# A decode kernel without its closing barrier, with its first transfers ahead of the entry barrier and w2 read in other pieces

## The chip, the core and the metric

The kernel runs on one core of one Trainium2 chip. The metric is the device time of one execution in microseconds (us). Beside it stands the *span* of a trace: the time from the first to the last instruction that the profile records. The time is a little longer than the span.

## The reference, cut to what matters

```python
x = A_x                                        # (8, 1, 576), bf16
g = sigmoid((x * gate_w).sum(-1))
# A: attention of one token over the last 2048 positions of a cache, 32 heads over 16 kv heads
q = x @ wq;  p = softmax(q @ k_cache[:, :, -2048:].T * 128**-0.5);  a = (p @ v_cache[:, :, -2048:]) @ wo
# B: an MLP
b = gelu(layernorm(x) @ w1 + b1) @ w2 + b2     # w1: (576, 4608), w2: (4608, 576)
out = g * a + (1 - g) * b                      # (8, 1, 576)
```

With 8 rows of activations there is little arithmetic. The two caches (8 x 16 x 2048 x 128 values each) and the weights have to come from HBM once: 154 MB.

## The kernel before

The kernel is a list of operations with dependencies, which a small planner puts in order for each engine and gives semaphores. SP issues nearly all transfers. They go into nine buffers of 16 KB in each partition, and one is issued as soon as the buffer that it needs is free.

```python
with ExitStack() as es:
    block = es.enter_context(nc.Block())         # closes with a barrier of all engines
    ...
    d_x   = dma("act", lambda e: e.dma_start(x_sb, x2), "x", ...)            # first transfer of ACT
    d_wqr = dma("sp", lambda e: e.dma_start(wq_r, A_wq[512:576, :]...), "wq", ...)  # first of SP
    d_wqm = dma("sp", lambda e: e.dma_start(wq_m..., A_wq[0:512, :]...), ...)       # second of SP
    ...
    # the last reads of the stream: w2, four blocks of 1152 rows, 9 rows to a partition
    src = B_w2[FCW * ci:FCW * ci + FCW, :].rearrange("(p j) n -> p (j n)", j=FJ)
    cuts = [0, 4, 7, 9] if ci == FC - 1 else [0, FJ]
    for n, (j0, j1) in enumerate(zip(cuts, cuts[1:])):
        d = dma("sp", lambda e: e.dma_start(dst[:, j0 * D:j1 * D], src[:, j0 * D:j1 * D]), ...)
        mms = [(hT[:, FJ * ci + j, :], dst[:, j * D:(j + 1) * D]) for j in range(j0, j1)]
        ...                                      # two matmuls of 288 columns for each row
    # then: two copies out of PSUM (DVE, ACT), two output transfers (SP, ACT), and
    add("sp", lambda e: None, deps=fin, name="final_wait", cost=0.05)

    P.schedule()
    @block.sync
    def _(e):
        P.emit("sp", e, eng_sems, dma_sems)
    ...                                          # the same for the other four engines
```

A program also begins with an entry barrier that is not in this text: each engine drains, GpSimd (POOL) sets four constants, and a semaphore releases all of them.

Of the kernel before, what the change touches and what calls it, by code (L numbers as in the profile page):

```python
# [12 lines left out]
ENGS = ("sp", "act", "pool", "dve", "pe")  # L13
# [25 lines left out]
class _Plan:  # L39
# [16 lines left out]
    def dma(self, eng, fn, semkey, nbytes, deps=(), name=None, after=(), prio=0):  # L56
        op = _Op(eng, fn, deps, name, self.DMA_ISSUE, after=after, is_dma=True, dma_sem=semkey, nbytes=nbytes, prio=prio)
        op.idx = len(self.all)
        self.all.append(op)
        return op  # L60
# [104 lines left out]
def _pst(t):  # L165
    return t.ap().ap[0][0]
# [13 lines left out]
def run_dma(nc, e, out, in_, shape=None):  # L180
    item = 2
    kw = {}
    if shape is not None:
        pst = shape[0]
        walk = shape[1]
        enc = []
        for step, num in reversed(walk[:-1]):
            parts, rest = divmod(step, pst)
            assert parts == 0 or rest == 0
            enc += [parts * 262144 + rest * item, num]  # L190
        enc += [0, 1] * (4 - len(enc) // 2)
        kw = dict(dst_dge_shape=enc, bass_dst_dge_shape=tuple(walk))
    return e.add_instruction(mybir.InstDMACopy(
        name=nc.get_next_instruction_name(), engine=e.engine, queue="qSPDynamicHW", mode="Copy",
        ins=e.lower_ap_dma(in_), outs=e.lower_ap_dma(out), **kw))


def build_kernel(nc, A_x, A_k_cache, A_v_cache, A_wq, A_wo, B_x, B_w1, B_b1, B_w2, B_b2, gate_w, out):
    B, Sq, D = A_x.shape
    _, Hkv, Sk, Dh = A_k_cache.shape  # L200
    Hq = A_wq.shape[1] // Dh
    F = B_w1.shape[1]
# [9 lines left out]
    FC, FJ = 4, 9  # L212
    FT = FC * FJ
    FCW = 128 * FJ
# [6 lines left out]
    out2 = out.rearrange("b s d -> (b s) d")  # L221

    with ExitStack() as es:
        block = es.enter_context(nc.Block())

        R = {}
        aoff = [0]

# [59 lines left out]
        AST = _pst(arena)  # L288
# [54 lines left out]
        def slot(s):  # L343
            return RAW[:, s * SE:(s + 1) * SE]
# [20 lines left out]
        eng_sems = {e: es.enter_context(nc.semaphore("sem_" + e)) for e in ENGS}  # L365
        dma_keys = ["x", "b", "b2", "wq", "w1", "out", "outb"] + ["s%d" % i for i in range(NSLOT)] + ["t%d" % i for i in range(4)]
        dma_sems = {k: es.enter_context(nc.semaphore("dma_" + k)) for k in dma_keys}

        P = _Plan()
        add, dma = P.add, P.dma  # L370
# [226 lines left out]
        def take_slot():  # L597
            n = n_slot[0]
            n_slot[0] += 1
            return (n + 6) % NSLOT  # L600
# [157 lines left out]
        def m2_chunk(ci):  # L758
            s = take_slot()
            dst = slot(s)[:, 0:FJ * D]  # L760
            src = B_w2[FCW * ci:FCW * ci + FCW, :].rearrange("(p j) n -> p (j n)", j=FJ)
            cuts = [0, 4, 7, 9] if ci == FC - 1 else [0, FJ]
            ops = []
            for n, (j0, j1) in enumerate(zip(cuts, cuts[1:])):
                d = dma("sp", (lambda j0=j0, j1=j1: lambda e: e.dma_start(dst[:, j0 * D:j1 * D], src[:, j0 * D:j1 * D]))(),  # L765
                        ("t%d" % n) if ci == FC - 1 else ("s%d" % s), 128 * (j1 - j0) * D * 2, deps=slot_free[s] if n == 0 else [], name="d_w2_%d_%d" % (ci, n), after=last_dma[-1:])
                last_dma.append(d)
                mms = [(hT[:, FJ * ci + j, :], dst[:, j * D:(j + 1) * D]) for j in range(j0, j1)]
                ops.append(AccGroup("m2_%d_%d" % (ci, n), mms, [o_hT, d], cost=0.25 * (j1 - j0), after=o_m2[-1:]).op)
                o_m2.append(ops[-1])  # L770
            slot_free[s] = ops

        pv_hist = []
        for kind, i in stream:
            {"K": k_unit, "V": v_unit, "W": wo_chunk, "M": m2_chunk, "B": bias}[kind](i)
# [11 lines left out]
        add("sp", lambda e: None, deps=fin, name="final_wait", cost=0.05)  # L787

        P.schedule()
        @block.sync  # L790
        def _(e):
            P.emit("sp", e, eng_sems, dma_sems)

        @block.gpsimd
        def _(e):
            P.emit("pool", e, eng_sems, dma_sems)

        @block.vector
        def _(e):
            P.emit("dve", e, eng_sems, dma_sems)  # L800

        @block.tensor
        def _(e):
            P.emit("pe", e, eng_sems, dma_sems)

        @block.scalar
        def _(e):
            P.emit("act", e, eng_sems, dma_sems)

    return P  # L810

# [1 line left out]
def bass_gated_mix__sliding_block_cached__mixer_channel_mlp__decode_kernel(  # L813
    nc: bass.Bass,
    A_x: bass.AP,
    A_k_cache: bass.AP,
    A_v_cache: bass.AP,
    A_wq: bass.AP,
    A_wo: bass.AP,
    B_x: bass.AP,  # L820
    B_w1: bass.AP,
    B_b1: bass.AP,
    B_w2: bass.AP,
    B_b2: bass.AP,
    gate_w: bass.AP,
    out: bass.AP,
):
    build_kernel(nc, A_x, A_k_cache, A_v_cache, A_wq, A_wo, B_x, B_w1, B_b1, B_w2, B_b2, gate_w, out)
# [28 lines left out]
```

## Time and profile before

| | before |
|---|---|
| time, median of the first 3 runs | 369.21 us |
| span of the profiled run, and its time | 367.5 us, 369.27 us |
| bytes read, mean rate over the span | 154 MB, 421 GB/s |
| busy: PE, DVE | 69%, 57% |

The first view is the DMA part of the profile. The digits are the busy share of the 16 DMA engines in 40 equal slices of the span, in tenths (9 is 90% or more); below them stands what they moved.

```profile
DMA  8999999999999999999999999999999999999994
GB/s 345 428 408 428 428 427 433 432 426 432 435 430 432 422 427 430 432 439 431 426 430 428 422 438 427 430 426 428 433 430 430 428 431 426 433 428 432 418 424 191
DMA packets 11851, 154.59 MB, mean 421 GB/s; under 512 B 1292, under 2 KB 1332, under 8 KB 3000
```

Between the ends the stream runs at about 430 GB/s without a hole. So the time is: when the stream starts, plus bytes over rate, plus what follows the last byte. Only the first slice (345) and the last (191) leave something to gain.

The start, from the timeline of SP's queue (start and duration in us, engine, line, what) and from the windows view (a stretch in us, its length, busy time of PE, PE's weight loads, DVE, ACT, POOL, then PE's clock, DMA share and GB/s):

```profile
0.79 0.39 SPq L401 DMA_DIRECT2D arena<-in_A_wq_dram  x1
1.24 0.42 SPq L402 DMA_DIRECT2D arena<-in_A_wq_dram  x1
1.70 0.42 SPq L404 DMA_DIRECT2D arena<-in_B_w_dram  x1
...
1.10:1.70 0.60, 0.00 (x0) 0.00 (x0) 0.00 (x0) 0.00 (x0) 0.56 (x3) 1.00 0.00 0
1.70:2.30 0.60, 0.00 (x0) 0.00 (x0) 0.00 (x0) 0.00 (x0) 0.59 (x5) 1.00 0.82 150
```

Nothing is issued for 0.79 us, and nothing moves until about 1.7 us.

The tail, from the chain of waits that ended last (start, duration, what):

```profile
297.09 32.53 DMA arena<-in_A_v_cache_dram
329.62 0.04 issue
329.66 1.08 PE ps L700 x16
...
333.71 30.42 DMA arena<-in_B_w_dram
364.13 0.04 issue
364.18 0.53 PE ps L559 x6
364.71 0.02 issue
364.73 0.43 PE ps L559 x4
...
365.28 0.45 DVE arena L783
```

The second piece of w2's last block (three rows, six matmuls) releases PE at 364.13; the last piece (two rows, four matmuls) follows. The same moments on PE's weight loads, whose bracket gives the idle time before them and what ended it:

```profile
364.17 0.22 PEld L559 LDWEIGHTS ps<-arena 128*8 128x8 bf16 x6 [0.97 <-DMA arena<-in_B_w_dram]
364.73 0.09 PEld L559 LDWEIGHTS ps<-arena 128*8 128x8 bf16 x4 [0.34 <-DMA arena<-in_B_w_dram]
```

And the end, from the records of the line that opened the closing block (first and last start in us); the output transfer of SP is issued at 365.75:

```profile
L223 SPq COMPARE_BRANCH  x1: 42/42/42, 367.1 to 367.1; - x1
L223 SPq DRAIN  x1: 13/13/13, 367.3 to 367.3; - x1
L223 SPq EVENT_SEMAPHORE  x1: 17/17/17, 367.5 to 367.5; - x1
L223 ACTq EVENT_SEMAPHORE  x1: 17/17/17, 367.5 to 367.5; - x1
```

The view of SP's waits shows (us in total, times, longest):

```profile
SPq L223 <- DMA out_dram<-arena: 0.2, 1, 0.2
```

The packed trace holds the times of *landing signals*: 16 for a large transfer, as many as there are DMA engines. That each signal is that of one engine is inferred from this number. In this trace the waits end with the last of them (the chain's 329.62 and 364.13 are such last signals). The views print no single signals, so they were read from the file. ACT's half of the output landed at 366.92, SP's half at 367.12.

### The profile page before, as it was taken

Reading aid. Unit: us, or ns where it says so; the run is one execution under the profiler, and the core shown is the slowest. Engines: PE = TensorE matmul, PEld = TensorE weight load, DVE = VectorE, ACT = ScalarE, POOL = GpSimd, SP = SyncE. Lnnn points to the kernel's source line nnn. Section 1 sums busy time; section 2 is a strip of 40 time slices with the busy share of each in tenths; the row PEclk is TensorE's granted clock in tenths of the full one; section 3 lists DMA queues with packets and bytes.
Section 4 is the critical chain, followed back from the end, with each engine's and each line's share of the span. In section 5 each row is a group of like instructions: output and inputs, shape, how many; then the busy total and the mean of one; then the engine's idle time right before and its main releaser. Section 6 shows DMA issues by size and latency. Waiting matters only on the chain.

```text
span 367.5 us, 4111 instructions
## 1 busy us (share of the span) xinstructions
PE 254.8 (69%) x1815; PEld 87.3 (24%) x1429; DVE 210.1 (57%) x253; ACT 47.8 (13%) x117; POOL 37.6 (10%) x163
## 2 busy tenths in 40 slices
PE   0349982895598398673986397765966396865995
PEld 0339200131123032010321032111311031214552
DVE  0704699797667754459654764478544864473000
ACT  1010002100300310003000300003100300003200
POOL 7020010011012001000101001010101000000000
PEclk9999998799689879887898879696988789795559
DMA  8999999999999999999999999999999999999994
GB/s 345 428 408 428 428 427 433 432 426 432 435 430 432 422 427 430 432 439 431 426 430 428 422 438 427 430 426 428 433 430 430 428 431 426 433 428 432 418 424 191
DMA packets 11851, 154.59 MB, mean 421 GB/s; under 512 B 1292, under 2 KB 1332, under 8 KB 3000
## 3 DMA queue, kind: packets, MB, share of 16 engines
q1 hardware_dynamic: 11776, 154.29, 98.6%
q8 instruction: 13, 0.21, 0.2%
q10 hardware_dynamic: 56, 0.03, 0.1%
q14 instruction: 6, 0.05, 0.0%
HBM read 154.31 MB, written 0.01 MB: 420 GB/s over the span
## 4 chain that ended last, share of the span: by engine, by line
DMA 74%; DVE 12%; PE 11%; SPq 1%; ACT 1%; issue 1%; DVEq 0%; ACTq 0%
DMA arena<-in_A_k_cache_dram 50%; DMA arena<-in_B_w_dram 15%; DMA arena<-in_A_v_cache_dram 9%; DVE arena L660 9%; PE ps L173 5%; PE ps L516 2%; PE ps L677 1%; DVE arena L605 1%; PE ps L700 1%; SPq L765 1%; ACT arena L619 1%; DVE arena L624 1%; PE ps L518 1%; PE ps L715 1%; DVE arena L614 0%
## 5 line engine op out<-in xcount | busy, mean ns | idle before, releaser
L660 DVE STREAM_TRANSPOSE arena<-arena 128x2048 f32<-128x2048 f32 x64 | 145.2, 2297 | 78.9 <-DMA arena<-in_A_k_cache_dram 71.5
L173 PE MATMUL ps<-arena 128*128 128x512 bf16 x401 | 134.4, 445 | 15.3 <-DVE arena L660 9.8
L677 PE MATMUL ps<-arena 128*128 128x512 bf16 x115 | 51.8, 450 | 16.7 <-DVE arena L660 16.6
L709 ACT ACTIVATE arena<-ps 128x512 f32<-128x512 f32 x32 | 19.1, 598 | 196.7 <-PE ps L700 196.7
L677 PEld LDWEIGHTS ps<-arena 128*128 128x128 bf16 x128 | 14.6, 114 | 125.8 <-issue 66.8
L715 PE MATMUL ps<-arena 128*128 128x8 f32 x256 | 36.9, 275 | 8.7 <-ACT arena L709 7.7
L653 POOL COPY arena<-arena 32x32 bf16<-32x32 bf16 x128 | 26.0, 203 | 159.2 <-PE ps L173 144.6
L715 PEld LDWEIGHTS ps<-arena 128*128 128x128 f32 x256 | 35.6, 217 | 22.4 <-ACT arena L709 16.4
L700 PE MATMUL ps<-arena 128*32 128x512 bf16 x512 | 36.7, 413 | 6.0 <-DMA arena<-in_A_v_cache_dram 6.0
L669 PE MATMUL ps<-arena 128*128 128x512 bf16 x6 | 3.5, 585 | 37.8 <-DVE arena L624 37.8
L605 DVE TENSOR_REDUCE arena<-ps 128x1 f32<-128x2048 f32 x8 | 18.3, 2282 | 15.5 <-PE ps L173 15.5
L619 ACT ACTIVATE arena<-ps,arena 128x512 bf16<-128x512 f32 x32 | 21.6, 686 | 41.4 <-DVE arena L614 41.4
L700 PEld LDWEIGHTS ps<-arena 128*32 128x32 bf16 x512 | 11.3, 100 | 39.8 <-issue 24.1
L624 DVE STREAM_TRANSPOSE arena<-arena 128x512 bf16<-128x512 bf16 x32 | 19.8, 674 | 0.9 <-ACT arena L619 0.9
L733 POOL TENSOR_TENSOR arena<-arena 128x16 bf16<-128x16 f32 x15 | 4.0, 267 | 142.3 <-ACT arena L725 142.3
L516 PE MATMUL ps<-arena 128*128 128x8 bf16 x144 | 10.9, 201 | 4.5 <-DMA arena<-in_B_w_dram 4.5
L559 PE MATMUL ps<-arena 128*8 128x288 bf16 (+1 forms) x140 | 11.6, 315 | 1.9 <-DMA arena<-in_B_w_dram 1.7
L516 PEld LDWEIGHTS ps<-arena 128*128 128x128 bf16 x144 | 10.8, 159 | 5.0 <-DMA arena<-in_B_w_dram 5.0
L669 PEld LDWEIGHTS ps<-arena 128*128 128x128 bf16 x8 | 0.9, 107 | 45.1 <-DVE arena L624 45.1
L733 DVE TENSOR_TENSOR arena<-ps,arena 128x16 bf16<-128x16 f32 x1 | 0.2, 229 | 19.4 <-PE ps L715 19.4
L438 PE MATMUL ps<-arena 8*128 8x8 bf16 x8 | 0.5, 168 | 13.5 <-DVE arena L411 9.8
L631 DVE RECIPROCAL arena<-ps 128x32 f32<-128x32 f32 x8 | 2.9, 358 | 10.5 <-PE ps L629 10.5
(83 smaller groups left out, 95.6 us busy)
## 6 DMA issues: line engine op xcount, KB each, us to landing
arena<-in_A_k_cache_dram SPq DMA_DIRECT2D x32, 2048.0 KB, 35.8
arena<-in_A_v_cache_dram SPq DMA_DIRECT2D x32, 2048.0 KB, 36.7
arena<-in_B_w_dram SPq DMA_DIRECT2D x1, 4608.0 KB, 24.3
arena<-in_A_wq_dram SPq DMA_DIRECT2D x1, 4096.0 KB, 13.1
arena<-in_B_w_dram SPq DMA_DIRECT2D x3, 1296.0 KB, 33.9
arena<-in_B_w_dram SPq DMA_DIRECT2D x2, 576.0 KB, 28.7
arena<-in_A_wq_dram SPq DMA_DIRECT2D x1, 512.0 KB, 3.7
arena<-in_B_w_dram SPq DMA_DIRECT2D x1, 432.0 KB, 30.4
```

The lines of the kernel that those rows point to most:

```text
L173: return e.add_instruction(mybir.InstMatmult(name=nc.get_next_instruction_name(), engine=mybir.EngineType.PE, ins=[e.lower_ap(rhs), e.lowe ...
L516: ins = e.matmul(out_, lhsT, yT[:, kt, :], start=(kt == 0), stop=False)
L559: ins = e.matmul(ps[32 * j:32 * j + 8, BK_ACC, 0:JN], lhsT, rhs[:, JN * j:JN * j + JN], start=False, stop=True, skip_group_check=True, til ...
L605: mx = add("dve", lambda e: e.tensor_reduce(out=k(MX), in_=ps[:, 0:4, :].rearrange("p a n -> p (a n)"), axis=AXL.X, op=ALU.max), deps=[qk_ ...
L619: return e.activation(out=Pm[:, 512 * c:512 * c + 512], in_=ps[:, c, :], func=ACTF.Exp, bias=k(NB), scale=SCALE, accum_out=k(SUM + c))
L624: pts.append(add("dve", (lambda c=c: lambda e: e.transpose(bass.AP(arena, offset=aoffs("PT") + 2048 * (g % 2) + 128 * c, ap=[[AST, 128], [ ...
L653: return e.tensor_copy(dst, src)
L660: tr = add("dve", (lambda h=h, kb=kb: lambda e: e.transpose(bass.AP(arena_f, offset=foffs("KT") + kb * 2048, ap=[[AST // 2, 128], [1, 2048]]),
L677: mm = e.matmul(*args, start=False, stop=last) if rc == 0 else held_matmul(nc, e, *args, stop=last)
L700: mm = e.matmul(ps[c:c + 32, BK_OS[i % 2], :], PT[:, g % 2, 512 * q + 32 * t:512 * q + 32 * t + 32], slot(s)[:, 512 * t:512 * t + 512], st ...
L709: u_ev[i] = add("act", lambda e: e.activation(out=EV[:, i % 2, :], in_=ps[:, BK_OS[i % 2], :], func=ACTF.Copy), deps=[prev] + ([u_sum[i - ...
L715: mm = e.matmul(ps[:, BK_S, OC + 16 * (item % 2) + 8 * (q % 2):OC + 16 * (item % 2) + 8 * (q % 2) + 8], EV[:, i % 2, 128 * r:128 * r + 128 ...
```

## The change

Its intent: drop the barrier at the end, since SP waits for the output anyway; issue the first two transfers of SP and the first of ACT before the entry barrier; read w2 in fewer, longer pieces (36 consecutive rows, 41472 B, written to four partitions, where before each partition's 9 rows, 10368 B, were a piece); and leave less work behind the last piece. The diff, with cuts marked:

```diff
-        block = es.enter_context(nc.Block())
...
-            cuts = [0, 4, 7, 9] if ci == FC - 1 else [0, FJ]
+            cuts = [0, 4, 8, 9] if ci == FC - 1 else [0, FJ]
...
-                d = dma("sp", (lambda ...: e.dma_start(dst[:, j0 * D:j1 * D], src[:, j0 * D:j1 * D]))(),
+                def w2_fn(e, j0=j0, j1=j1):
+                    if ci < FC - 1:
+                        rows = bass.AP(B_w2.tensor, offset=FCW * ci * D, ap=[[4 * FJ * D, 32], [1, 4 * FJ * D]])
+                        return run_dma(nc, e, dst, rows, (AST, ((4 * AST, 32), (AST, 4), (1, FJ * D))))
+                    return e.dma_start(dst[:, j0 * D:j1 * D], src[:, j0 * D:j1 * D])
+                d = dma("sp", w2_fn,
...
-        @block.sync
-        def _(e):
-            P.emit("sp", e, eng_sems, dma_sems)
-        ...                                   (and four more)
+        entry = nc.cur_bb.bb.instructions
+        n_entry = len(entry)
+        handles = {"sp": nc.sync, "act": nc.scalar, "pool": nc.gpsimd, "dve": nc.vector, "pe": nc.tensor}
+        for eng in ENGS:
+            P.emit(eng, handles[eng], eng_sems, dma_sems)
+        for etype, count in ((mybir.EngineType.SP, 2), (mybir.EngineType.Activation, 1)):
+            first = [i for i in entry[n_entry:] if i.engine == etype][:count]
+            assert all(isinstance(i, mybir.InstDMACopy) for i in first)
+            for i in first:
+                entry.remove(i)
+            at = next(n for n, i in enumerate(entry) if i.engine == etype and isinstance(i, mybir.InstDrain))
+            entry[at:at] = first
```

More of the change, by code (lines that the diff above doesn't have):

```diff
@@ L761, in m2_chunk @@
             src = B_w2[FCW * ci:FCW * ci + FCW, :].rearrange("(p j) n -> p (j n)", j=FJ)
-            cuts = [0, 4, 7, 9] if ci == FC - 1 else [0, FJ]
+            cuts = [0, 4, 8, 9] if ci == FC - 1 else [0, FJ]
             ops = []
             for n, (j0, j1) in enumerate(zip(cuts, cuts[1:])):
-                d = dma("sp", (lambda j0=j0, j1=j1: lambda e: e.dma_start(dst[:, j0 * D:j1 * D], src[:, j0 * D:j1 * D]))(),
+                def w2_fn(e, j0=j0, j1=j1):
[4 more added lines that the diff above has]
+                d = dma("sp", w2_fn,
                         ("t%d" % n) if ci == FC - 1 else ("s%d" % s), 128 * (j1 - j0) * D * 2, deps=slot_free[s] if n == 0 else [], name="d_w2_%d_%d" % (ci, n), after=last_dma[-1:])
@@ L789, in build_kernel @@
         P.schedule()
-        @block.sync
-        def _(e):
-            P.emit("sp", e, eng_sems, dma_sems)
-        @block.gpsimd
-        def _(e):
-            P.emit("pool", e, eng_sems, dma_sems)
-        @block.vector
-        def _(e):
-            P.emit("dve", e, eng_sems, dma_sems)
-        @block.tensor
-        def _(e):
-            P.emit("pe", e, eng_sems, dma_sems)
-        @block.scalar
-        def _(e):
-            P.emit("act", e, eng_sems, dma_sems)
+        entry = nc.cur_bb.bb.instructions
[10 more added lines that the diff above has]
+            entry[at:at] = first
     return P
```

## The prediction

> **What bounds the kernel.** The reads from HBM. The page's header of its DMA part gives 154.6 MB in a span of 367.5 us, a mean of 421 GB/s; the slices show the DMA engines 90% busy or more in all but the first and the last. In stretches that hold only cache reads the windows view gives 430 to 432 GB/s. PE is busy 69%, DVE 57%. Transfers take about 36 us from issue to landing, so the queue always holds many: an engine a little sooner or later changes nothing between. The time is (start of the stream) + (bytes / rate) + (tail after the last byte). The change touches only these ends and 5.3 MB of w2.
>
> **Start.** In the timeline the first wq transfer issues at 0.79 us, behind the entry barrier (SP drains at 0.0, the barrier's semaphore comes at 0.7, after POOL's four constants and PE's late drain at 0.3). The first bytes move in the window 1.5 to 2.0. Hoisted, the two wq transfers issue at about 0.05 and x on ACT at about 0.1. The issues last 0.39 and 0.42 us, so SP reaches the barrier at about 0.9 and everybody leaves it at about 1.0 instead of 0.75. wq holds over 10 us of stream, so w1 (issued near 1.1, was 1.70) follows without a gap. The whole stream moves 0.6 to 0.7 us earlier, and it is full until the end, so this reaches the end: -0.65.
>
> **End.** The final wait is met at 366.9; then come a branch (367.1), SP's drain (367.3), POOL's semaphores (367.4) and the release (367.5). All of it goes: -0.5. The Trainium skill ("Runtime: NRT & Kernel Launch", the preamble/postamble breakdown) lists a barrier after the kernel anyway; time minus span, 1.7 us, should stay. No run yet shows that.
>
> **w2.** Blocks 0 to 2 (4.0 MB, 9.3 us) read at 427 GB/s in the windows 351 to 358, against 431 for the cache. A row group of 9 is 10368 B, 40.5 x 256 B, so every second descriptor starts off a 256 B boundary; 36 rows are 41472 B, 162 x 256. The Trainium skill ("DMA: Bandwidth & Descriptors", "How a descriptor splits into AXI transactions") says a misaligned start fetches from the boundary below. About 1% of 9.3 us: -0.1.
>
> **Last block.** In the chain the second piece releases PE at 364.18: 6 matmuls 0.53 us, then 4 in 0.43, then DVE at 365.28. PE waits for data there, but the last piece (two rows) was in by 364.7. With four and one rows the second piece lands about 0.2 to 0.3 us later and then PE has 8 + 2 matmuls at 0.09 to 0.1 us: about 0.1 us worse to nothing. Between 361 and 364 the DMA share falls from 0.8 to 0.3: some engines finish 2 to 3 us before the slowest.
>
> **Sum.** -0.65 - 0.5 - 0.1 + 0.05 = -1.2 us: 368.0 us, range 367.3 to 368.7, a gain of 0.3%. Faster by over 2%: 0.01; within 2%: 0.98; slower by over 2%: 0.01.
>
> **What would show it.** First transfer at under 0.2 us and first bytes near 0.9; landing of the last w2 piece 0.6 to 0.8 us earlier; span near 366.3, with SP's final wait its last record; windows over w2 at about 431 GB/s; the final matmuls 8 then 2.
>
> **What would make it wrong.** Transfers issued before the barrier might start no sooner; the order of rows in w2 may spread unevenly over the 16 engines, lengthening the skewed tail (up to +1 us), or shorten it (-1 us); the metric may not count the barrier's part of the end.

## The result, and the profile after

| | before | after | difference |
|---|---|---|---|
| time, median of 6 runs | 369.18 us (369.00 to 369.29) | 367.61 us (367.29 to 367.81) | -1.57 |
| ratio | | 0.9958 (0.9945 to 0.9970) | |
| profiled run: span | 367.5 | 366.2 | -1.3 |
| profiled run: time | 369.27 | 367.52 | -1.75 |
| profiled run: time minus span | 1.77 | 1.32 | -0.45 |

The ratio is that of the fast runs, and not quite that of the medians. The gain is 0.4%: by the yardstick of 2% the time is the same, but the two ranges do not touch.

The profiled run after is one of the six. In those six, time minus span is 1.32, 1.2, 1.2, 1.29, 1.2 and 1.21, on average 1.24; the spans run from 366.0 to 366.6. So one profile of this kernel tells the span only to some 0.3 us either way, and the small terms below have to be read with that in mind. Of before a span is on record for the profiled run alone. These spans are rounded to 0.1 us; the packed traces have 367.54 and 366.23 for the two profiled runs, with which time minus span is 1.73 and 1.29.

The stream after, in the same view as before:

```profile
DMA  9999999999999999999999999999999999999994
GB/s 371 445 398 426 437 429 429 432 431 429 429 428 431 424 428 431 433 429 429 431 431 435 415 433 429 431 428 433 429 429 429 431 431 429 429 429 433 421 455 179
DMA packets 11563, 154.59 MB, mean 422 GB/s; under 512 B 1292, under 2 KB 1460, under 8 KB 3000
```

The 288 packets that are gone are the 3 x 96 fewer read pieces of w2. The body is as fast as it was. The start:

```profile
0.00 0.40 SPq L399 DMA_DIRECT2D arena<-in_A_wq_dram  x1
0.46 0.41 SPq L400 DMA_DIRECT2D arena<-in_A_wq_dram  x1
1.27 0.33 SPq L402 DMA_DIRECT2D arena<-in_B_w_dram  x1
...
0.50:1.10 0.60, 0.00 (x0) 0.00 (x0) 0.00 (x0) 0.00 (x0) 0.00 (x0) 1.00 0.00 0
1.10:1.70 0.60, 0.00 (x0) 0.00 (x0) 0.00 (x0) 0.00 (x0) 0.43 (x1) 1.00 0.79 198
```

The first issue is 0.79 us earlier. The first bytes before fall between 1.7 and 1.8 and those after between 1.1 and 1.2. But these are not bytes of the same transfer. The DMA view of 1.70 to 1.82 us before holds packets of ACT's queue alone, whose first transfer is x; by the packet records of the trace, wq's first bytes move at 1.82 before and at 1.11 after. So wq's first bytes are 0.71 us earlier: they come 1.1 us after its issue, where it took 1.0 behind the barrier. Issuing x early gained nothing by itself: it was issued at 0.12 instead of 0.79, but ACT's queue moved its first bytes at 2.05 instead of 1.74. SP leaves the barrier at 1.27, not at 0.79, because both issuing engines now come late to it and their drains are longer; the records of the entry barrier (durations in ns, then starts in us) show it:

```profile
L838 ACTq DRAIN  x1: 138/138/138, 0.8 to 0.8; - x1
L838 SPq DRAIN  x1: 125/125/125, 0.9 to 0.9; - x1
L838 SPq EVENT_SEMAPHORE  x1: 17/17/17, 1.2 to 1.2; - x1
```

That costs nothing, since the 4.7 MB of wq feed the stream until long after w1 is issued.

The tail of the chain of waits after:

```profile
297.28 31.38 DMA arena<-in_A_v_cache_dram
328.66 0.04 issue
328.70 1.07 PE ps L698 x16
...
332.79 30.60 DMA arena<-in_B_w_dram
363.39 0.04 issue
363.43 0.80 PE ps L557 x10
...
364.35 0.45 DVE arena L786
```

And the weight loads of the same moment:

```profile
363.43 0.46 PEld L557 LDWEIGHTS ps<-arena 128*8 128x8 bf16 x10 [1.20 <-DMA arena<-in_B_w_dram]
```

All ten matmuls of the second and the last piece run off one release, at 363.39; by its landing signals the last piece came at 363.70, while PE was still at the second. The kernel then ends on SP's wait for the output. The transfer is issued at 364.83, and this is the last record of the trace (the second start of the line is that of its last record):

```profile
L153 SPq EVENT_SEMAPHORE  x39: 17/17/202, 40.4 to 366.0; - x39
```

There is no record of a closing block any more. By the landing signals, ACT's half of the output landed at 366.01 and SP's at 366.21.

Put side by side, the 1.75 us between the two profiled runs split into three stretches without a rest:

| stretch | before | after | difference |
|---|---|---|---|
| start of the span to the issue of the output on SP | 365.75 | 364.83 | -0.92 |
| issue of the output to the end of the span | 1.75 | 1.37 | -0.38 |
| time minus span | 1.77 | 1.32 | -0.45 |

### The profile page after: what moved, and what is told of

Its sections match the earlier page's. It is cut to its first block, busy times and chain, and to the rows that moved or that the text cites. A ratio compares the mean times of both kernels' runs of the same rounds, so it can differ in the third digit from the quotient of the medians.

```text
span 366.2 us, 4124 instructions
## 1 busy us (share of the span) xinstructions
PE 265.5 (72%) x1837; PEld 89.3 (24%) x1429; DVE 210.4 (57%) x253; ACT 47.8 (13%) x117; POOL 37.5 (10%) x163
## 4 chain that ended last, share of the span: by engine, by line
DMA 65%; PE 17%; DVE 15%; SPq 1%; issue 1%; DVEq 0%
DMA arena<-in_A_k_cache_dram 41%; DMA arena<-in_B_w_dram 15%; DVE arena L658 11%; DMA arena<-in_A_v_cache_dram 9%; PE ps L173 8%; PE ps L675 3%; PE ps L514 2%; DVE arena L603 2%; PE ps L698 1%; DVE arena L622 1%; SPq L767 1%; PE ps L713 1%; PE ps L516 1%; PE ps L557 1%; DVE arena L612 0%
## 5 line engine op out<-in xcount | busy, mean ns | idle before, releaser
L173 PE MATMUL ps<-arena 128*128 128x512 bf16 x408 | 140.2, 459 | 0.0
L675 PE MATMUL ps<-arena 128*128 128x512 bf16 x128 | 58.4, 457 | 20.4 <-DVE arena L658 20.2
L667 PE MATMUL ps<-arena 128*128 128x512 bf16 x8 | 4.7, 586 | 41.6 <-DVE arena L622 41.6
L557 PE MATMUL ps<-arena 128*8 128x288 bf16 (+1 forms) x140 | 12.6, 342 | 0.9 <-DMA arena<-in_B_w_dram 0.9
```

The costliest lines, as they stand in the source:

```text
L173: return e.add_instruction(mybir.InstMatmult(name=nc.get_next_instruction_name(), engine=mybir.EngineType.PE, ins=[e.lower_ap(rhs), e.lowe ...
L557: ins = e.matmul(ps[32 * j:32 * j + 8, BK_ACC, 0:JN], lhsT, rhs[:, JN * j:JN * j + JN], start=False, stop=True, skip_group_check=True, til ...
L675: mm = e.matmul(*args, start=False, stop=last) if rc == 0 else held_matmul(nc, e, *args, stop=last)
```

## The experiments

None gave a result. So everything after this section that goes beyond the two traces is argued and not shown by an experiment, and is called so. The plan stands here, since a reader can learn from it which run would tell what apart.

So the 36 row reads alone could not have been tried, and every experiment had wo read by a plain pattern:

```diff
-            src = bass.AP(A_wo.tensor, offset=128 * h0 * D, ap=[[4 * D, 32], [128 * D, WO_CH], [1, 4 * D]])
-            d = dma("sp", lambda e: run_dma(nc, e, dst[:, :, 0:D], src, (AST, ((4 * AST, 32), (WOP, WO_CH), (AST, 4), (1, D)))),
+            src = A_wo[128 * h0:128 * (h0 + WO_CH), :].rearrange("(t p) c -> p t c", p=128)
+            d = dma("sp", lambda e: e.dma_start(dst[:, :, 0:D], src),
```

**The control**, before with that edit alone. Expected:

> The control of all the following runs. The kernel before, with wo read by plain patterns of 1152 B instead of 4608 B, because new kernels may not set the shape registers that the longer reads (of wo, and of w2 in the change) need. If short reads cost nothing: 369.2 us. If they cost 5 to 10% of the 11 us in which wo is read: 369.7 to 370.3 us. Time minus span 1.7 us as before.

Not measured.

**No closing barrier alone.** The edit on top of the control:

```diff
-        block = es.enter_context(nc.Block())
-        @block.sync ... (five engines)
+        handles = {"sp": nc.sync, "act": nc.scalar, "pool": nc.gpsimd, "dve": nc.vector, "pe": nc.tensor}
+        for eng in ENGS:
+            P.emit(eng, handles[eng], eng_sems, dma_sems)
```

It was to decide where the 0.45 us outside the span come from. Expected:

> The control without the closing barrier alone. Theory 1 (the four other engines finish early, so that less is left to do after the last record): span 0.4 us shorter, time minus span 1.25 instead of 1.7, time 0.8 to 0.9 us less than the control. Theory 2 (time minus span shrinks because of the transfers ahead of the entry barrier): span 0.4 us shorter, time minus span still 1.7, time 0.4 us less.

Without its control, the readings were chosen so that they do not depend on wo's reads:

> The kernel before without the closing barrier; nothing hoisted, w2 and its last block as before. wo is read by plain patterns of 1152 B, because new kernels may not set the shape registers that the longer reads need; that may cost 0 to 1.1 us of stream, so the two readings that decide are free of the stream: the records after the final wait, and time minus span. Theory 1 (the other engines finish early, so that less is left to do after the last record): the last record is SP's final wait, and time minus span is 1.2 to 1.3 as in the kernel after, against 1.7 before. Theory 2 (time minus span shrinks because of the transfers ahead of the entry barrier): the last record is SP's final wait, and time minus span stays 1.7. Time: 368.3 to 369.4 us under theory 1, 368.8 to 369.9 under theory 2.

Not measured.

**The first transfers ahead of the entry barrier alone**, with the closing barrier kept:

```diff
+        entry = nc.cur_bb.bb.instructions          # before the block is opened
         block = es.enter_context(nc.Block())
...
             P.emit("sp", e, eng_sems, dma_sems)
+            hoist(mybir.EngineType.SP, 2)          # moves the first two of this body ahead of SP's entry drain
...
             P.emit("act", e, eng_sems, dma_sems)
+            hoist(mybir.EngineType.Activation, 1)
```

> The control with the first two SP transfers and the first ACT transfer ahead of the entry barrier, closing barrier kept. Theory 1: first bytes at 1.1 instead of 1.7 us, span 0.6 us shorter, time minus span 1.7, time 0.6 us less than the control. Theory 2: span 0.6 us shorter, time minus span 1.25, time 1.0 to 1.1 us less.

Not measured.

**The last block in pieces of four, four and one rows alone:**

```diff
-            cuts = [0, 4, 7, 9] if ci == FC - 1 else [0, FJ]
+            cuts = [0, 4, 8, 9] if ci == FC - 1 else [0, FJ]
```

> The control with the last block of w2 cut 4, 4, 1 instead of 4, 3, 2. My prediction's step: 0 to 0.1 us longer, PE's last matmuls 8 and 2 after the second piece lands. Rival, from the trace after, where the end of PE moved by 0.93 us while the stream began 0.6 us earlier: 0.1 to 0.3 us shorter.

Not measured. The 0.6 us of this text is the move of the first bytes of any queue; the stream itself moved by more, and the landing signals below speak against the rival.

Two more kernels would tell more. In one, all five engines would wait for the output, without a closing barrier: if time minus span came back to 1.7 there, theory 1 would hold. The other would add 24 reads of 1.3 MB from w2 to the stream, all of 10368 B pieces, with starts that are all, half or never a multiple of 256 B, to make an effect of alignment large enough to measure.

## Why the prediction was right or wrong

The total was right: 368.0 was said, with 367.3 to 368.7, and 367.61 was measured. Of the terms of the sum, the start was nearly right, the last block was right, w2's was said too large, and the end was split wrongly: a part of it lay where the prediction expected nothing.

**What bounds the kernel: consistent with both traces.** The slices between the ends are near 430 GB/s in both, and what changed lies at the ends: the first slice rose from 345 to 371 GB/s.

**The start, said -0.65: right in mechanism, measured -0.75.** The issue moved by 0.79 us; wq's first bytes moved by 0.71 us. Whether that reaches the end can be followed along the stream. Wherever DVE waits for a cache read to land, the trace gives the moment of landing. Two such moments in DVE's timeline before (start and duration in us, what, and in the bracket the idle time that the landing ended):

```profile
32.39 4.51 DVE L660 STREAM_TRANSPOSE arena<-arena 128x2048 f32<-128x2048 f32 x2 [10.37 <-DMA arena<-in_A_k_cache_dram]
319.95 4.50 DVE L660 STREAM_TRANSPOSE arena<-arena 128x2048 f32<-128x2048 f32 x2 [5.21 <-DMA arena<-in_A_k_cache_dram]
```

And the same two after:

```profile
31.61 4.50 DVE L658 STREAM_TRANSPOSE arena<-arena 128x2048 f32<-128x2048 f32 x2 [8.75 <-DMA arena<-in_A_k_cache_dram]
319.00 4.51 DVE L658 STREAM_TRANSPOSE arena<-arena 128x2048 f32<-128x2048 f32 x2 [5.22 <-DMA arena<-in_A_k_cache_dram]
```

The first is 0.78 us earlier after, the other 0.95. These are moments of the slowest DMA engine, since a wait ends with the last of the 16 signals. Over all transfers of K, V and wo this last signal's lead wanders between 0.29 and 1.37 us. The mean of the 16 signals does not: its lead lies between 0.72 and 0.75 us in all of these transfers but one (0.85). So the lead of the start is kept through the whole body, as predicted, and it is 0.75 us.

At the end of the stream the slowest signal leads by 0.96 us, 0.21 more than the mean, because in this run the slowest DMA engine lagged less behind the others. Nothing in the traces ties that to the change. It looks like luck of the profiled run: its span is 366.2, while the six runs after have 366.35 on average.

**w2 in 36 rows, said -0.1: about -0.02 in this pair.** The prediction gave as its test that windows over w2 read 431 instead of 427 GB/s. That test fails as a test, as the windows after show:

```profile
347.00:351.00 4.00, 3.29 (x28) 2.23 (x24) 0.00 (x0) 0.60 (x1) 0.00 (x0) 0.50 1.23 508
351.00:354.00 3.00, 2.29 (x16) 1.68 (x8) 0.00 (x0) 0.60 (x1) 0.00 (x0) 0.50 1.00 429
354.00:358.00 4.00, 4.00 (x33) 1.83 (x35) 0.23 (x1) 0.00 (x0) 0.00 (x0) 0.50 0.88 373
```

508 GB/s is far above anything that the stream sustains, and it comes from the way of counting: the view gives a packet's bytes to the window in which the packet starts. Counted so, the packet records give these 508, 429 and 373; spread over each packet's duration they give 415, 428 and 428. The landing signals are a better measure. From the last transfer before w2 to the third block of long reads, the lead of the mean signal grows from 0.74 to 0.76 us (that of the slowest from 0.92 to 0.96). From the landing of V that releases PE near 329 to the last landing of w2 it is 35.06 us before (329.62 to 364.68) and 35.04 after (328.66 to 363.70). So the long reads brought some 0.02 to 0.04 us here and not 0.1; in a single pair that is hardly more than nothing. The packet records do show the expected 1%: 10368 B took 391.6 ns on average before (384 packets) and 41472 B took 1552.4 after (96 packets), 0.9% less for each byte. Why most of this does not reach the landings is not shown. The argument by alignment rests on the Trainium skill, "DMA: Bandwidth & Descriptors", section "How a descriptor splits into AXI transactions": a piece that does not start on a 256 B boundary fetches from the boundary below. That this is what makes the short pieces slower, no run here shows.

**The last block, said 0 to 0.1 us worse: right, 0.05 us worse.** It was said that with four and one rows the second piece would land 0.2 to 0.3 us later, and that PE would then have ten matmuls behind it. Here are the last landings of the two traces:

| last landing signal of, or end of | before | after | lead of after |
|---|---|---|---|
| w2's last block, first piece (four rows in both) | 362.82 | 361.86 | 0.96 |
| second piece (three rows before, four after) | 364.13 | 363.39 | 0.74 |
| last piece (two rows before, one after) | 364.68 | 363.70 | 0.98 |
| PE | 365.16 | 364.23 | 0.93 |

Against its neighbours the second piece lands 0.22 to 0.24 us later after the change. The last landing leads by 0.98, like the stream before it, so the cut did not move it by more than some 0.02 us. From the last landing to the end of PE it is 0.48 us before and 0.53 after: 0.05 worse, as the sum had it.

A reading from the release of PE misleads here. From that release to the end of PE it is 1.03 us before (364.13 to 365.16) and only 0.84 after (363.39 to 364.23), because before the weight loads of the last four matmuls stood idle for 0.34 us until the last piece was there, and after the ten ran without a break. But what ended sooner had also begun later, by the 0.22 us. All this is one pair of traces; a run of the cut alone is missing.

In both traces the DMA engines finish unevenly: the 16 signals of the last piece are spread over 3.3 us before and 3.1 after, where the prediction said 2 to 3. Here are windows over the last four microseconds of the stream before:

```profile
360.60:361.60 1.00, 0.12 (x2) 0.09 (x4) 0.00 (x0) 0.00 (x0) 0.00 (x0) 1.00 0.92 369
361.60:362.60 1.00, 1.00 (x18) 0.63 (x14) 0.00 (x0) 0.00 (x0) 0.00 (x0) 1.00 0.64 248
362.60:363.60 1.00, 0.81 (x12) 0.27 (x8) 0.00 (x0) 0.00 (x0) 0.00 (x0) 1.00 0.37 136
363.60:364.60 1.00, 0.42 (x6) 0.18 (x6) 0.00 (x0) 0.00 (x0) 0.00 (x0) 1.00 0.13 51
```

And after:

```profile
359.70:360.70 1.00, 1.00 (x14) 0.57 (x10) 0.00 (x0) 0.00 (x0) 0.00 (x0) 0.65 0.94 383
360.70:361.70 1.00, 1.00 (x22) 0.70 (x16) 0.00 (x0) 0.00 (x0) 0.00 (x0) 1.00 0.76 293
361.70:362.70 1.00, 0.85 (x14) 0.27 (x8) 0.00 (x0) 0.00 (x0) 0.00 (x0) 1.00 0.39 143
362.70:363.70 1.00, 0.27 (x6) 0.20 (x8) 0.00 (x0) 0.00 (x0) 0.00 (x0) 1.00 0.12 42
```

The next-to-last column falls in the same way in both: the change left the uneven finish nearly as it was. This is a thing left to gain at this end of the kernel: after, the mean of the 16 signals is at 362.33 and the last at 363.70, so that an even finish would be worth up to 1.4 us (an estimate from these two numbers).

Together the start, w2 and the last block were said to bring 0.70 us, and the profiled pair shows 0.92 up to the issue of the output: 0.75 from the start, 0.21 from the slowest DMA engine and 0.02 from w2, less 0.05 for the last block.

**The end, said -0.5, all of it inside the span: the wrong split.** Inside the span, from the issue of the output to the last record, 0.38 us went. The records of the closing block are gone, as predicted. But the prediction took the wait at 366.9 for the moment when the output was in. That was ACT's half alone; SP's landed at 367.12, and the branch waited for it. From this landing to the end of the span it is 0.42 us before (367.12 to 367.54) and 0.02 after (366.21 to 366.23). So the barrier held 0.40 us, and the wait for SP's half stays: after, the last record of the wait lasts 202 ns where before none of this line on SP is longer than 28.

Outside the span another 0.45 us went, and the prediction had said "time minus span, 1.7 us, should stay". This is the step that failed. It is not an accident of the profiled run: 1.2 to 1.3 in all six runs after, against 1.77 in the profiled run before. So the end of the program brought -0.38 and -0.45, if the second belongs to the end, and not -0.5. The two errors of the prediction, the end's (0.83 against 0.50) and that of the stretch before it (0.92 against 0.70), go in the same direction; they add up to the difference between 1.75 us in the profiled pair and the 1.20 that were said. Between the medians it is 1.57 against 1.20. The prediction's span, 366.3, was met: the six runs have 366.35 on average. That is in part luck, since the small errors inside it (start, w2, barrier, slowest engine) nearly cancel; the miss of the total lies in time minus span.

Two explanations of the 0.45 us stay open. By the first, the other four engines finish their part of the program early when there is no barrier to hold them, and less is left to do once SP is through: before, ACT, DVE and PE are held until the release at 367.5, after, they end with their own work, DVE with its copy at 364.80 and ACT with the issue of its output at 365.07. The Trainium skill, "Runtime: NRT & Kernel Launch", section "The ~15µs preamble/postamble breakdown", lists a barrier for all engines behind the kernel (about 1.5 us) and a reset of semaphores behind it, which might fit; the traces do not show that stretch. By the second, the transfers ahead of the entry barrier move something that lies before the first record. The traces give one hint on this. The records of the other engines in the entry barrier stand where they stood against the start of the span: POOL's first constant starts at 0.31 us before and 0.30 after, DVE's drain at 0.12 in both, PE's at 0.31 in both. So SP's first record (its drain before, its first transfer after) has not moved against the other engines, and anything that became shorter before it became shorter for all of them. That speaks for the first explanation and does not show it. The change does both things at once, and the run without the closing barrier alone would have told them apart.

## What to carry to other kernels

In a kernel whose DMA queue never runs dry, a transfer that is issued earlier at the start is worth its lead at the end: the 0.75 us that it brought, as the mean over the 16 landing signals, were still there 320 us later. Follow the landings, and the mean of their signals beside the last one, since the last shows the slowest engine's luck too. Measure what a cut of the last piece costs from the last landing, and not from the release of an earlier piece that the cut moved itself. Read the time beside the span: here a quarter of the gain lay where no record of the profile does, and a prediction from the records alone could not see it. When the terms of a change are as small as the spread of the runs (0.5 us here), a single pair of traces settles only those that are an issue time, a landing that can be followed, or a record that is gone; the others need runs of one part alone, and it is better to say so than to name a cause.

## What the Trainium skill lacked or had wrong

- "DMA: Bandwidth & Descriptors", section "Specifications", gives a first-byte latency of about 0.6 us for transfers of SP and ACT, but not from where it counts. For the first transfer of SP it was 1.0 us before (0.79 to 1.82) and 1.1 after (0.00 to 1.11) from the start of the issue; from the end of the 0.4 us issue, 0.6 and 0.7.
- "Runtime: NRT & Kernel Launch" lists the stages around a kernel, but does not say what of them is hidden when engines end at different times. Time minus span was 1.77 us in a run with a closing barrier in the kernel and 1.2 to 1.3 in six runs without one and with the first transfers ahead of the entry barrier; which of the two did it is open.
- No page says what a drain of the program itself lasts behind a transfer that its engine has just issued: at the entry barrier SP's took 7 ns and ACT's 8 before, but 125 and 138 ns after.
- "Perfetto Trace Analysis" does not warn that a rate over a short window depends on where long packets are counted: with packets of 41472 B (1.55 us each) a window of 4 us showed 508 GB/s by their starts and 415 by their durations, in a stream that sustains some 430.
